# A gated FFN behind an inducing-point attention: the l factor on ScalarE, a thinner first output projection, a split last block

## The chip, the cores and the metric

The kernel runs on one core of one Trainium2 chip. The metric is the device time of one execution in microseconds (us); of the runs of a kernel the median counts. The core's engines are named as in the profile: PE (TensorE matmul; PEld is its weight load), DVE (VectorE), ACT (ScalarE), POOL (GpSimd) and SP (SyncE, which here only issues DMAs).

## The reference

Two blocks stand one behind the other. The first is attention through 32 inducing points `I`: `h = softmax(scale · I xᵀ) x` over all 12416 rows of a batch, then `out = softmax(scale · x hᵀ) h` for each row. The second is a gated FFN over all 49664 rows. Cut to what matters:

```python
B, N, m, C = (4, 12416, 32, 128)          # d_ff = 1536
def mab(q, kv):
    s = scale * (q @ kv.transpose(0, 2, 1))
    s = s - s.max(-1, keepdims=True)
    a = np.exp(s)
    a /= a.sum(-1, keepdims=True) + 1e-09
    return a @ kv
x = mab(x, mab(I, x)).reshape(B * N, C)
gate = 1.0 / (1.0 + np.exp(-(x @ w_gate)))
out = gate * (x @ w_val) @ w_out           # float32
```

## The kernel before

**Stage 1 and the first combine.** A batch is 97 chunks of 128 rows, taken in groups of 16 chunks and one group of one. For batch 0 all of stage 1 runs alone at the start: scores of the 32 inducing points against a group (L178), the negated maximum (L190), the exponential (L203), a transpose on PE (L216) that DVE copies out (L222), and the weighted sum of x rows (L236). Each group has its own maximum, so the groups are put together at the end (L559 to L625). There `ml` is the extreme of a partition's late groups, `wl` their weights (L562, ACT), `lsum` the weighted sum of the denominators (L596 and L598, DVE) and `hpart` the weighted sum of the numerators (four `scalar_tensor_tensor` at L603, DVE, each reading what the one before it wrote). The four 32-partition strips have separate extremes; POOL brings them together in `quad` (L566 to L576), ACT and POOL copy the result to all strips as `top` (L581, L583), and ACT forms the strip weight `w4` (L586) and `e32w` = `e32`·`w4` (L588). `e32l` = `e32`·`w4`·`lsum` is formed by DVE (L613) between the third and the fourth L603. Two fp32 matmuls then add up the strips: `l_ps` from `e32l` (L622) and `h_ps` from `hpart` and `e32w` (L624). `l_inverse` (L281, L283) and `h_take` (L288) give `hT`, from which the scores of the second attention (L362) and `hw`, h times both weight matrices (L294), are made. In this way the attention's second product and the two first FFN products become one matmul with 32 rows of contraction.

**The main loop.** The output is cut into 97 blocks of four chunks, 512 rows (the last block holds the one left-over chunk of each batch). A block has 12 slices of d_ff, done in 8 steps of alternately two slices and one: 776 steps in all. For step t, `product(t)` issues the value matmuls (`v_ps`, L696) and one DVE instruction `u = (t16 + 1) · v` (L717); `gate(t + 2)` issues the gate matmuls (`g_ps`, L696) and the tanh on ACT (L711). Steps with two slices use PSUM tiles of two banks (`g2`, `v2`), those with one slice one bank (`g1`, `v1`); each exists once, so the next value matmul into `v2` waits until DVE has read the last. Two steps are called a slot here: after the even step `beside` issues stage 1 and stage 2 work of what is to come, and after the odd step `project` issues output matmuls. One output chunk is four 128-column matmuls into `acc` (L733) that use one slice of one step's `u` as weights; a block takes 12 of them, after which ACT scales `acc` into `o32` (L745) and SP stores 256 KB (L748, for the last block L750). `project` does at most three chunks a slot, four if more than three wait, and stops behind a block's last chunk; in a steady state it is three a slot, twelve matmuls. The order of the instructions on each engine is the order in which this Python code issues them.

**PSUM.** The eight banks are `g2` (2), `v2` (2), `g1`, `v1`, `acc` and `m`; `m` serves the work of `beside`.

Of the kernel before, what the change touches and what calls it, by code (L numbers as in the profile page):

```python
# [9 lines left out]
F32 = mybir.dt.float32  # L10
# [3 lines left out]
ALU = mybir.AluOpType  # L14
AX = mybir.AxisListType

P = 128
GC = 16
BC = 4
# [2 lines left out]
S1_FIRST = 7  # L22
S2_LEAD = 20
COMBINE_LAG = 6


@with_exitstack
def kernel(
# [9 lines left out]
    nc = tc.nc  # L38
    B, N, C = x.shape
    m = inducing.shape[0]  # L40
    F = moe_w_gate.shape[1]
    NJ = F // P
# [11 lines left out]
    const = ctx.enter_context(tc.tile_pool(name="const", bufs=1))  # L54
# [7 lines left out]
    op = ctx.enter_context(tc.tile_pool(name="op", bufs=4))  # L62
# [3 lines left out]
    ps = ctx.enter_context(tc.tile_pool(name="ps", bufs=1, space=bass.MemoryType.PSUM))  # L66

    xv = x.rearrange("b (p j) c -> b p j c", p=P)
    ov = out.rearrange("(b p j) c -> b p j c", b=B, p=P)
    ov0 = out.rearrange("(b p j) c -> p j b c", b=B, p=P)  # L70
# [18 lines left out]
    def x_transpose_dma(b, s):  # L89
# [16 lines left out]
        out=identf[:],  # L106
        in_=identf[:],
# [21 lines left out]
    e32 = const.tile([P, m], F32, tag="e32")  # L129
# [9 lines left out]
    NS = len(groups)  # L139
    arrival = [0, NG] + list(range(1, NG))  # L140
    at_col = {s: p for p, s in enumerate(arrival)}
    EARLY = NS - 4
    nml = const.tile([P, 1 + NS - EARLY], F32, tag="nml")
    l1l = const.tile([P, 1 + NS - EARLY], F32, tag="l1l")
# [23 lines left out]
    def s1_dims(s):  # L168
        n = groups[s][1]
        ng = min(4, n)  # L170
        return ng, n // ng, 32 * ng
# [40 lines left out]
    def s1_turn_pe(b, s, a1T, tag="m"):  # L212
        ng, w, R = s1_dims(s)
        aT = ps.tile([P, 4, P], F16, tag=tag, name="aT_ps")
        for k in range(w):
            nc.tensor.transpose(aT[:, k, 0:R], a1T[0:R, ts(k, P)], ident[0:R, 0:R])  # L216
        return aT

    def s1_turn_copy(s, aT):
        ng, w, R = s1_dims(s)  # L220
        a1 = s1p.tile([P, 4, P], F16, tag="a1")
        nc.vector.tensor_copy(out=a1[:, 0:w, 0:R], in_=aT[:, 0:w, 0:R])  # L222
        return a1
# [6 lines left out]
    def s1_sum(b, s, a1, tag):  # L230
        c0, n = groups[s]
        ng, w, R = s1_dims(s)
        hp = ps.tile([P, C], F32, tag=tag, name="hp_ps")
        for k in range(w):
            for g in range(ng):
                nc.tensor.matmul(  # L236
                    hp[32 * g : 32 * g + 32, :],
                    a1[:, k, 32 * g : 32 * g + 32],
                    xn[b][:, c0 + g * w + k, :],
                    start=(k == 0),  # L240
                    stop=(k == w - 1),
                )
        summed[b] += 1
        if b == 0 and at_col[s] > EARLY:
            return hp
        nc.scalar.copy(out=hsts[b % 2][0:R, at_col[s], :], in_=hp[0:R, :])
# [25 lines left out]
    def add_tree(x, k, out=None):  # L272
        while k > 1:
            r = k // 2
            o = x[:, 0:r] if k > 2 or out is None else out
            nc.gpsimd.tensor_tensor(out=o, in0=x[:, 0:r], in1=x[:, k - r : k], op=ALU.add)
            k -= r
# [25 lines left out]
    def combine(b):  # L303
# [5 lines left out]
        for g in range(4):  # L309
            nc.gpsimd.tensor_copy(out=quad[:, g, :], in_=nm1[32 * g : 32 * g + 32, :])  # L310
        for _ in range(COMBINE_LAG):
            yield
# [20 lines left out]
        add_tree(hx, NS)  # L333
        for _ in range(COMBINE_LAG):
            yield
# [165 lines left out]
    a1T, a1 = {}, {}  # L501
    nm1, l1, hst = nm1s[0], l1s[0], hsts[0]
    for p in range(-2, NS - 3):
# [11 lines left out]
        if p + 1 == EARLY - 1:  # L515
# [3 lines left out]
                out=nml[:, 0:1], in_=nm1[:, 0:EARLY], axis=AX.X, op=ALU.min  # L519
            )  # L520
            nc.scalar.activation(
                out=we[:], in_=nm1[:, 0:EARLY], func=AF.Exp, bias=nml[:, 0:1], scale=-1.0
            )
            lw = const.tile([P, EARLY], F32, tag="lwe")
# [21 lines left out]
    sc, sb, sa = arrival[-1], arrival[-2], arrival[-3]  # L546
# [8 lines left out]
    aT = s1_turn_pe(0, sa, a1T[sa])  # L555
# [5 lines left out]
    wl = const.tile([P, 1 + NS - EARLY], F32, tag="wl")  # L561
    nc.scalar.activation(out=wl[:], in_=nml[:], func=AF.Exp, bias=ml[:], scale=-1.0)  # L562
    nc.scalar.mul(out=hpart[0][:], in_=hpart[0][:], mul=wl[:, 0:1])
    quad = const.tile([m, 4], F32, tag="quad0")
    for g in range(4):
        nc.gpsimd.tensor_copy(out=quad[:, g : g + 1], in_=ml[32 * g : 32 * g + 32, :])  # L566
    nc.gpsimd.tensor_scalar(
        out=quad[:, 0:1],
        in0=quad[:, 0:1],
        scalar1=quad[:, 1:2],  # L570
        scalar2=quad[:, 2:3],
        op0=ALU.min,
        op1=ALU.min,
    )
    nc.gpsimd.tensor_scalar(
        out=quad[:, 0:1], in0=quad[:, 0:1], scalar1=quad[:, 3:4], scalar2=None, op0=ALU.min  # L576
# [7 lines left out]
    nc.gpsimd.dma_start(wo16[:], moe_w_out.rearrange("(j p) c -> p j c", p=P))  # L584
    w4 = const.tile([P, 1], F32, tag="w4")
    nc.scalar.activation(out=w4[:], in_=ml[:], func=AF.Exp, bias=top[:], scale=-1.0)  # L586
    e32w = const.tile([P, m], F32, tag="e32w")
    nc.scalar.mul(out=e32w[:], in_=e32[:], mul=w4[:])  # L588
    for g in range(3):
        x_load(1, g)  # L590

    a1[sa] = s1_turn_copy(sa, aT)
    a1[sb] = s1_turn_copy(sb, s1_turn_pe(0, sb, a1T[sb], "g2"))
    hps = [hst[:, EARLY, :], s1_sum(0, sa, a1[sa], "acc")[:]]
    lw = const.tile([P, 1 + NS - EARLY], F32, tag="lwl")
    nc.vector.tensor_mul(out=lw[:], in0=l1l[:], in1=wl[:])  # L596
    lsum = const.tile([P, 1], F32, tag="lsum0")
    nc.vector.reduce_sum(out=lsum[:], in_=lw[:], axis=AX.X)  # L598
    a1[sc] = s1_turn_copy(sc, s1_turn_pe(0, sc, a1T[sc], "v2"))
    hps.append(s1_sum(0, sb, a1[sb], "m")[:])  # L600
    hps.append(s1_sum(0, sc, a1[sc], "v1")[:])
    for k, hp in enumerate(hps):
        nc.vector.scalar_tensor_tensor(  # L603
            out=hpart[0][:],
            in0=hp,
            scalar=wl[:, 1 + k : 2 + k],
            in1=hpart[0][:],
            op0=ALU.mult,
            op1=ALU.add,
        )  # L610
        if k == len(hps) - 2:
            e32l = const.tile([P, m], F32, tag="e32l0")
            nc.vector.tensor_scalar(  # L613
                out=e32l[:],
                in0=e32[:],
                scalar1=w4[:],
                scalar2=lsum[:],
                op0=ALU.mult,
                op1=ALU.mult,
            )  # L620
    l_ps = ps.tile([P, m], F32, tag="g1", name="l_ps")
    nc.tensor.matmul(l_ps[:], ones[:], e32l[:], start=True, stop=True)  # L622
    h_ps = ps.tile([P, m], F32, tag="m", name="h_ps")
# [9 lines left out]
        out=nmx_a[:], in_=s2_a[:, 0:BC, :], axis=AX.X, op=ALU.max, negate=True  # L633
# [3 lines left out]
        out=low[:],  # L637
        in0=s2_a[:, 0:BC, :],
        in1=nmx_a[:].unsqueeze(2).to_broadcast((P, BC, m)),
        op=ALU.add,  # L640
# [34 lines left out]
    blocks = []  # L675
# [10 lines left out]
    NST = len(steps)  # L686
# [19 lines left out]
    def gate(t):  # L706
        if t < NST:
            st = steps[t]
            hidden_mm(st, "g")
            st["t"] = tp.tile([P, st["cnt"], 512], F16, tag=f"t{st['cnt']}", name="t16")  # L710
            nc.scalar.activation(out=st["t"][:], in_=st["g"][:], func=AF.Tanh, scale=0.5)  # L711

    def product(t):
        st = steps[t]
        hidden_mm(st, "v")
        st["u"] = up.tile([P, st["cnt"], 512], F16, tag=f"u{st['cnt']}", name="u16")
        nc.vector.scalar_tensor_tensor(  # L717
            out=st["u"][:], in0=st["t"][:], scalar=1.0, in1=st["v"][:], op0=ALU.add, op1=ALU.mult
        )

    acc = [None]
    queue = [(t, k) for t in range(NST) for k in range(steps[t]["cnt"])]
# [2 lines left out]
    def project(upto, now, room):  # L725
        while queue and queue[-1][0] < upto and room > 0:
            t, k = queue.pop()
            st = steps[t]
            j = st["j0"] + k
            if j == 0:  # L730
                acc[0] = ps.tile([P, BC, C], F32, tag="acc", name="acc_ps")
            for i in range(BC):
                nc.tensor.matmul(  # L733
                    acc[0][:, i, :],
                    st["u"][:, k, ts(i, P)],
                    wo16[:, j, :],
                    start=(j == 0 and i == 0),
                    stop=(j == NJ - 1),
                    skip_group_check=True,
                )  # L740
            room -= 1
            if j == NJ - 1:
                block = blocks[st["block"]]
                o32 = op.tile([P, BC, C], F32, tag="o32")
                nc.scalar.mul(out=o32[:], in_=acc[0][:], mul=0.5)  # L745
                if len(block) == 1:
                    b, c, nb = block[0]
                    nc.sync.dma_start(ov[b, :, c : c + nb, :], o32[:])  # L748
                else:
                    nc.sync.dma_start(ov0[:, 0, :, :], o32[:])  # L750
                if now < NST:
                    return

# [5 lines left out]
    for b in range(B):  # L759
        at = base[b]  # L760
        for s in range(1, NS):
            c, n = groups[s]
# [70 lines left out]
    def waiting(upto):  # L833
        n = 0
        for e in reversed(queue):
            if e[0] >= upto:
                break
            n += 1
        return n
# [3 lines left out]
    for t in range(NST):  # L843
        product(t)
        gate(t + 2)
        if t % 2 == 0:
            beside(t // 2)
        else:
            project(t - 1, t, 3 if waiting(t - 1) <= 3 else 4)
    project(NST, NST, 10**6)  # L850


# [28 lines left out]
```

## Time and profile before

| | |
|---|---|
| runs shown | 768.11, 768.52, 766.72 us; median 768.11 |
| profiled execution | 768.34 us, of which the span from first to last instruction is 766.5 |
| first value and gate matmuls of the main loop | 31.8 us from the span's start |
| last matmul, last eviction, last store issued | end at 762.34, 762.97 and 763.39 us |
| share of the span busy | DVE 96%, ACT 88%, PE 87%, POOL 36% |

The span splits into a start-up of about 32 us, in which stage 1 of batch 0 and the first combine run, the main loop of some 730 us, and a tail of 4.2 us behind the last matmul. In a line of the timeline the first number is the start, the second the length of the merged group, and the bracket tells the idle time of the engine ahead of it and what ended it. A row of a table of windows gives the window, its length, the busy time and the number of instructions of each engine, and then the granted PE clock, where 1.00 is full and 0.50 is half.

### The profile page before, as it was taken

The page shows a single profiled execution, that of the slowest core. Times are in us where ns is not written, and L with a number is a line of the kernel's source. Part 1 is how long each engine was busy: PE and PEld are TensorE (multiplying, and loading weights), DVE is VectorE, ACT ScalarE, POOL GpSimd, SP SyncE. Part 2 cuts the span into 40 slices and gives each one's busy share as a digit, 9 for nine tenths or more (in the row PEclk, how much of TensorE's full clock was granted, in tenths as well). Part 3 has the DMA queues.
Part 4 walks back from the last instruction along what each step waited for, and adds up shares of the span by engine and source line. Part 5 has one row for each costly group of instructions (what it writes and reads, how often), then busy time and mean ns, then how long its engine had stood idle before and what let it go on. Part 6 is the DMA issues. An engine that isn't in the chain of part 4 may idle for free.

```text
span 766.5 us, 20798 instructions
## 1 busy us (share of the span) xinstructions
PE 669.1 (87%) x8167; PEld 402.6 (53%) x8167; DVE 736.3 (96%) x911; ACT 672.4 (88%) x1008; POOL 275.7 (36%) x439
## 2 busy tenths in 40 slices
PE   6788889889888888989888888888998888888887
PEld 4445555555555455555555545555555555555554
DVE  4889999999999999999999999999999999999997
ACT  4689889899898989989998989989999989889896
POOL 3535050582350441545513504147335135135100
PEclk9689999999999999999999999999999999999999
DMA  8979752604249525244138342121221121231211
GB/s 168 154 144 181 149 83 84 112 29 98 71 92 178 115 63 112 57 97 86 49 78 158 88 89 63 49 57 36 78 57 49 52 68 41 58 69 34 67 43 43
DMA packets 117730, 65.16 MB, mean 85 GB/s; under 512 B 101344, under 2 KB 102016, under 8 KB 117632
## 3 DMA queue, kind: packets, MB, share of 16 engines
q1 hardware_dynamic: 112192, 49.94, 27.9%
q0 software_dynamic: 5440, 13.90, 11.1%
q8 instruction: 64, 1.05, 0.6%
q14 instruction: 34, 0.28, 0.1%
HBM read 27.80 MB, written 25.43 MB: 69 GB/s over the span
## 4 chain that ended last, share of the span: by engine, by line
DVE 34%; PE 28%; issue 20%; ACT 14%; POOL 4%; DMA 1%; ACTq 0%; DVEq 0%; POOLq 0%
DVE u L717 30%; PE acc_ps L733 11%; PE v_ps L696 11%; ACT t L711 10%; PE s_ps L362 2%; DVE nm L190 2%; DVE nmx L373 2%; ACT a1T L203 1%; PE g_ps L696 1%; ACT e L395 1%; ACT o L745 1%; PE xt_ps L494 1%; POOL near L427 1%; PE s_ps L386 1%; DMA xn<-in_x_dram 1%
## 5 line engine op out<-in xcount | busy, mean ns | idle before, releaser
L717 DVE SCALAR_TENSOR_TENSOR u<-t,v_ps 128x1024 f16<-128x1024 f16 (+1 forms) x776 | 692.2, 950 | 11.3 <-ACT t L711 3.4
L711 ACT ACTIVATE t<-g_ps 128x1024 f16<-128x1024 f32 (+1 forms) x776 | 598.2, 818 | 68.2 <-PE g_ps L696 53.8
L696 PE MATMUL v_ps<-a2r,hwt 32*128 32x512 f16 (+1 forms) x1188 | 292.8, 371 | 79.3 <-DVE u L717 76.3
L733 PE MATMUL acc_ps<-wo,u 128*128 128x128 f16 x4656 | 328.6, 220 | 1.1
L733 PEld LDWEIGHTS <-u 128*128 128x128 f16 x4656 | 262.7, 98 | 97.4 <-issue 95.6
L696 PE MATMUL g_ps<-a2r,hwt 32*128 32x512 f16 (+1 forms) x1188 | 296.1, 378 | 0.3
L696 PEld LDWEIGHTS <-hwt 32*128 32x128 f16 x2400 | 100.0, 91 | 214.6 <-issue 168.7
L377 POOL CAST hi<-nmx 128x16 bf16<-128x16 f32 (+2 forms) x28 | 5.5, 196 | 320.4 <-DVE nmx L373 288.1
L449 POOL TENSOR_TENSOR a2n<-e,rs 128x2048 f16<-128x2048 f16 (+2 forms) x28 | 86.9, 3105 | 8.3 <-DVE rs L421 3.5
L427 POOL TENSOR_TENSOR near<-sme,minus 128x16 f32<-128x16 f32 (+1 forms) x26 | 66.9, 2572 | 1.9
L745 ACT ACTIVATE o<-acc_ps 128x512 f32<-128x512 f32 x97 | 58.8, 606 | 4.1 <-PE acc_ps L733 4.1
L403 POOL TENSOR_TENSOR sum<-e 128x256 f32<-128x256 f16 (+1 forms) x27 | 16.2, 599 | 72.2 <-ACT e L395 72.2
L403 POOL TENSOR_TENSOR sum<-sum 128x128 f32<-128x128 f32 (+3 forms) x108 | 31.5, 292 | 8.5
L362 PEld LDWEIGHTS <-xT 128*128 128x128 f16 x388 | 13.6, 97 | 12.5 <-issue 12.4
L362 PE MATMUL s_ps<-hT,xT 128*128 128x32 f16 x388 | 18.2, 179 | 0.7 <-DVE hT L288 0.5
L373 DVE TENSOR_REDUCE nmx<-s_ps 128x16 f32<-128x512 f32 (+2 forms) x28 | 17.0, 607 | 0.0
L203 ACT ACTIVATE a1T<-s_ps,nm 128x512 f16<-128x512 f32 (+1 forms) x24 | 15.0, 627 | 1.7 <-DVE nm L190 1.7
L190 DVE TENSOR_REDUCE nm<-s_ps 128x1 f32<-128x512 f32 (+1 forms) x24 | 14.8, 615 | 0.9 <-PE s_ps L178 0.9
L83 POOL DMA_DIRECT2D xn<-in_x_dram x25 | 15.1, 613 | 1.1 <-POOLq L865 0.8
L395 ACT ACTIVATE e<-s_ps 128x512 f16<-128x512 f32 (+2 forms) x28 | 14.9, 533 | 0.6 <-PE s_ps L386 0.6
L498 ACT COPY xT<-xt_ps 128x1024 f16<-128x1024 f16 (+1 forms) x6 | 5.6, 940 | 8.1 <-PE xt_ps L494 8.1
L496 DVE COPY xT<-xt_ps 128x1024 f16<-128x1024 f16 (+2 forms) x8 | 4.7, 598 | 8.3 <-PE xt_ps L494 8.3
(105 smaller groups left out, 200.0 us busy)
## 6 DMA issues: line engine op xcount, KB each, us to landing
out_dram<-o SPq DMA_DIRECT2D x97, 256.0 KB, 2.4
xn<-in_x_dram POOLq DMA_DIRECT2D x19, 512.0 KB, 6.6
xn<-in_x_dram POOLq DMA_DIRECT2D x4, 544.0 KB, 6.3
a2r<-a2n SPq DMA_TRANSPOSE x29, 5.1
xn<-in_x_dram POOLq DMA_DIRECT2D x1, 384.0 KB, 13.9
wg<-in_moe_w_gate_dram POOLq DMA_DIRECT2D x1, 384.0 KB, 4.5
wv<-in_moe_w_val_dram POOLq DMA_DIRECT2D x1, 384.0 KB, 5.8
wo<-in_moe_w_out_dram POOLq DMA_DIRECT2D x1, 384.0 KB, 5.4
```

The lines of the kernel that those rows point to most:

```text
L190: nc.vector.tensor_reduce(out=nm[0:R, col], in_=s1[0:R, 0 : w * P], axis=AX.X, op=ALU.max, negate=True)
L203: nc.scalar.activation(out=a1T[0:R, 0 : w * P], in_=s1[0:R, 0 : w * P], func=AF.Exp, bias=nm[0:R, col], accum_out=l1[0:R, col],)
L362: nc.tensor.matmul(s2[:, j, :], xT[b][:, c + j, :], hT16[b][:], start=(j == 0), stop=whole and j == j1 - 1, skip_group_check=True,)
L373: nc.vector.tensor_reduce(out=nmx[:, 0:n], in_=s2[:, 0:n, :], axis=AX.X, op=ALU.max, negate=True)
L403: nc.gpsimd.tensor_tensor(out=d[:, 0:n, :], in0=src[:, :, 0:w], in1=src[:, :, w : 2 * w], op=ALU.add)
L427: nc.gpsimd.tensor_tensor(out=near[:, 0:n], in0=sme[:, 0:n], in1=minus1[:, 0:n], op=ALU.pow)
L449: eng.tensor_tensor(out=a2n[:, 0:n, :, :], in0=e.unsqueeze(2).to_broadcast((P, n, 4, m)), in1=rs.unsqueeze(2).unsqueeze(3).to_broadcast((P ...
L696: nc.tensor.matmul(pt[:, k, col : col + nb * P], hw[b][r : r + 32, j // 2, :], a2r[r : r + 32, o : o + nb, :].rearrange("p j t -> p (j t)" ...
L711: nc.scalar.activation(out=st["t"][:], in_=st["g"][:], func=AF.Tanh, scale=0.5)
L717: nc.vector.scalar_tensor_tensor(out=st["u"][:], in0=st["t"][:], scalar=1.0, in1=st["v"][:], op0=ALU.add, op1=ALU.mult)
L733: nc.tensor.matmul(acc[0][:, i, :], st["u"][:, k, ts(i, P)], wo16[:, j, :], start=(j == 0 and i == 0), stop=(j == NJ - 1), skip_group_chec ...
L745: nc.scalar.mul(out=o32[:], in_=acc[0][:], mul=0.5)
```

## The change

Three edits.

1. **First combine.** The PE transposes, copies and sums of the groups `sa` and `sb`, and with them `lw` and `lsum`, are written ahead of the `quad` part. ACT then forms `e32s` = `e32`·`lsum` ahead of its copies of `top`, and `e32l` = `e32s`·`w4` right behind `w4` and ahead of `e32w`. The DVE instruction that formed `e32l` is gone. The orders on PE and POOL stay the same; DVE loses the one instruction; ACT gains two of 128x32.
2. **Output chunks.** While t < COLD = 8, `project` does at most one chunk a slot. The first odd step, t = 1, has no chunk yet, so three slots (t = 3, 5, 7) have one chunk in place of three. The chunks left over are done in later slots of four: on PE the slots from t = 3 on have 4, 4, 4, 16, 16, 4, 16, 16, 16, 16, 16, 16 output matmuls, where each had 12; from t = 27 on both orders are the same.
3. **Last block.** The last step's `u` is made by two DVE instructions of 256 columns. The last block accumulates in two PSUM banks (`acc` for the first two chunks, `m` for the other two). ACT evicts one and SP stores it, DVE evicts the other and ACT's queue issues its store.

```diff
+COLD = 8
...
     nc.scalar.mul(out=hpart[0][:], in_=hpart[0][:], mul=wl[:, 0:1])
+    a1[sa] = s1_turn_copy(sa, aT)
+    a1[sb] = s1_turn_copy(sb, s1_turn_pe(0, sb, a1T[sb], "g2"))
+    hps = [hst[:, EARLY, :], s1_sum(0, sa, a1[sa], "acc")[:]]
+    lw = const.tile([P, 1 + NS - EARLY], F32, tag="lwl")
+    nc.vector.tensor_mul(out=lw[:], in0=l1l[:], in1=wl[:])
+    lsum = const.tile([P, 1], F32, tag="lsum0")
+    nc.vector.reduce_sum(out=lsum[:], in_=lw[:], axis=AX.X)
+    e32s = const.tile([P, m], F32, tag="e32s")
+    nc.scalar.mul(out=e32s[:], in_=e32[:], mul=lsum[:])
...
     nc.scalar.activation(out=w4[:], in_=ml[:], func=AF.Exp, bias=top[:], scale=-1.0)
+    e32l = const.tile([P, m], F32, tag="e32l0")
+    nc.scalar.mul(out=e32l[:], in_=e32s[:], mul=w4[:])
     e32w = const.tile([P, m], F32, tag="e32w")
...
-        if k == len(hps) - 2:
-            e32l = const.tile([P, m], F32, tag="e32l0")
-            nc.vector.tensor_scalar(
-                out=e32l[:],
-                in0=e32[:],
-                scalar1=w4[:],
-                scalar2=lsum[:],
-                op0=ALU.mult,
-                op1=ALU.mult,
-            )
...
-        nc.vector.scalar_tensor_tensor(
-            out=st["u"][:], in0=st["t"][:], scalar=1.0, in1=st["v"][:], op0=ALU.add, op1=ALU.mult
-        )
+        cuts = [0, 512] if t < NST - 1 else [0, 256, 512]
+        for c, e in zip(cuts, cuts[1:]):
+            nc.vector.scalar_tensor_tensor(
+                out=st["u"][:, :, c:e],
...
             if j == 0:
-                acc[0] = ps.tile([P, BC, C], F32, tag="acc", name="acc_ps")
+                acc[0] = [ps.tile([P, BC, C], F32, tag="acc", name="acc_ps")]
+                if st["block"] == len(blocks) - 1:
+                    acc[0].append(ps.tile([P, BC, C], F32, tag="m", name="acc_ps"))
             for i in range(BC):
                 nc.tensor.matmul(
-                    acc[0][:, i, :],
+                    acc[0][(i // 2) % len(acc[0])][:, i, :],
...
-                    start=(j == 0 and i == 0),
+                    start=(j == 0 and i in ((0, 2) if len(acc[0]) > 1 else (0,))),
...
+            if t == NST - 1:
+                o32 = op.tile([P, BC, C], F32, tag="o32")
+                nc.scalar.mul(out=o32[:, 0:2], in_=acc[0][0][:, 0:2], mul=0.5)
+                nc.sync.dma_start(ov0[:, 0, 0:2, :], o32[:, 0:2])
+                nc.vector.tensor_scalar_mul(out=o32[:, 2:4], in0=acc[0][1][:, 2:4], scalar1=0.5)
+                nc.scalar.dma_start(ov0[:, 0, 2:4, :], o32[:, 2:4])
+            elif j == NJ - 1:
...
-            project(t - 1, t, 3 if waiting(t - 1) <= 3 else 4)
+            project(t - 1, t, 1 if t < COLD else 3 if waiting(t - 1) <= 3 else 4)
```

More of the change, by code (lines that the diff above doesn't have):

```diff
@@ L590 @@
         x_load(1, g)
[L592 to L598, printed above, removed]
     a1[sc] = s1_turn_copy(sc, s1_turn_pe(0, sc, a1T[sc], "v2"))
@@ L716, in product @@
         st["u"] = up.tile([P, st["cnt"], 512], F16, tag=f"u{st['cnt']}", name="u16")
-        nc.vector.scalar_tensor_tensor(
-            out=st["u"][:], in0=st["t"][:], scalar=1.0, in1=st["v"][:], op0=ALU.add, op1=ALU.mult
-        )
+        cuts = [0, 512] if t < NST - 1 else [0, 256, 512]
+        for c, e in zip(cuts, cuts[1:]):
+            nc.vector.scalar_tensor_tensor(
+                out=st["u"][:, :, c:e],
+                in0=st["t"][:, :, c:e],
+                scalar=1.0,
+                in1=st["v"][:, :, c:e],
+                op0=ALU.add,
+                op1=ALU.mult,
+            )
     acc = [None]
@@ L741, in project @@
             room -= 1
-            if j == NJ - 1:
+            if t == NST - 1:
[5 more added lines that the diff above has]
+            elif j == NJ - 1:
                 block = blocks[st["block"]]
                 o32 = op.tile([P, BC, C], F32, tag="o32")
[L745 to L750, printed above, removed]
+                nc.scalar.mul(out=o32[:], in_=acc[0][0][:], mul=0.5)
+                b, c, nb = block[0]
+                nc.sync.dma_start(ov[b, :, c : c + nb, :], o32[:])
                 if now < NST:
```

## The prediction

> **What bounds the kernel now.** I read the page's busy times and its clock row first, then windows laid along the changes of the clock, then the timelines of DVE and PE where it is half, the chain of waits through the first combine, and the last instructions.
>
> ```profile
> PE 669.1 (87%) x8167; PEld 402.6 (53%) x8167; DVE 736.3 (96%) x911; ACT 672.4 (88%) x1008; POOL 275.7 (36%) x439
> ...
> PEclk9689999999999999999999999999999999999999
> ...
> 25.45:35.69 10.24, 7.01 (x55) 2.95 (x55) 7.75 (x21) 5.06 (x10) 5.26 (x7) 0.50 1.01 162
> 35.69:39.11 3.42, 3.42 (x32) 1.90 (x31) 2.77 (x5) 1.88 (x4) 1.01 (x3) 0.50 1.14 197
> 39.11:42.52 3.41, 3.41 (x21) 1.50 (x22) 2.70 (x3) 2.56 (x4) 0.00 (x0) 0.50 1.21 224
> 42.52:45.93 3.41, 2.82 (x38) 1.78 (x36) 2.86 (x4) 2.88 (x6) 2.15 (x6) 1.00 0.62 113
> ```
>
> The main loop is DVE's (96%), and all three edits lie outside it: in the start-up, in the first slots and in the tail. The windows show the granted clock at 0.50 from 25.45 to 42.52 us, and there, from 35.69 on, PE is busy all the time (3.42 of 3.42) while DVE is not. So the first slots are PE's.
>
> ```profile
> 38.77 1.82 DVE L717 SCALAR_TENSOR_TENSOR u<-t,v_ps 128x1024 f16<-128x1024 f16 x2 [0.65 <-PE g_ps L696]
> 41.13 1.22 DVE L717 SCALAR_TENSOR_TENSOR u<-t,v_ps 128x1024 f16<-128x1024 f16 x1 [0.54 <-PE g_ps L696]
> 42.64 0.69 DVE L717 SCALAR_TENSOR_TENSOR u<-t,v_ps 128x512 f16<-128x512 f16 x1 [0.28 <-ACT e L395]
> 43.75 2.99 DVE L717 SCALAR_TENSOR_TENSOR u<-t,v_ps 128x1024 f16<-128x1024 f16 x3 [0.43 <-PE g_ps L696]
> ...
> 39.02 1.46 PE L733 MATMUL acc_ps<-wo,u 128*128 128x128 f16 x12
> 40.41 0.61 PE L696 MATMUL v_ps<-a2first,hwt 32*128 32x512 f16 x2
> ...
> 746.22 0.84 PE L733 MATMUL acc_ps<-wo,u 128*128 128x128 f16 x12
> 747.07 0.39 PE L696 MATMUL v_ps<-a2r,hwt 32*128 32x512 f16 x2
> ```
>
> DVE stood idle 0.65 + 0.54 + 0.28 + 0.43 = 1.90 us there. Twelve output matmuls hold PE for 40.41 - 39.02 = 1.39 us at half clock (116 ns each) and 747.07 - 746.22 = 0.85 at full clock less the gap before the next group, which I take as 65 ns each.
>
> **Edit 1, the first combine.** The chain of waits runs through the fourth L603, `l_ps` and the inverse to `hT`:
>
> ```profile
> 25.81 0.06 DVE e32l L613
> 25.86 0.06 issue
> 25.93 0.45 DVE hpart L603
> 26.37 0.11 issue
> 26.48 0.62 PE l_ps L622 x2
> ...
> 24.84 0.39 ACT L581 COPY top<-quad 32x1 f32<-32x1 f32 x2 [0.44 <-POOL quad L575]
> 25.32 0.30 ACT L586 ACTIVATE w<-ml,top 128x1 f32<-128x1 f32 x1
> 25.65 0.32 ACT L588 ACTIVATE e32w<-e,w 128x32 f32<-128x32 f32 x1
> ```
>
> The row of L613 gives 0.615 us for the one `e32l`: from 25.72 it ends at 26.33, and `l_ps` starts 0.15 behind it, at 26.48. After the change `e32l` takes `e32w`'s place on ACT, 25.65 to 25.97 by that row, and `l_ps` starts at 26.11: -0.37. What else `hT` needs does not hold it: the fourth L603 loses 0.08 (from 25.93 to 25.85) and ends at 26.26; `e32w` is pushed behind `e32l` to about 26.25; `h_ps` goes 0.42 behind `l_ps`, at 26.53, and ends at 27.14, before `li` at 27.33. The added wait is `e32s` on ACT for `lsum`, which DVE ends at 24.37. Behind it in ACT's queue stand the two copies of `top`, `w4`, `e32l`, `e32w` and, from 29.01, `e_a`. `e32s` would run 24.42 to 24.74 (0.32 as `e32w`), and the copies wait for POOL's `quad` until 24.84 in any case; the cover is 0.10 us, and what exceeds it delays `w4` one for one. The instructions written earlier keep their order on PE, DVE and POOL, so no queue but ACT's changes. Bounds: -0.40 to -0.08 (the L603 share alone). I take -0.37, because `l_ps` then waits for ACT and for nothing DVE ends later.
>
> **Edit 2, the first slots.** The half-clock slot around 40 us is PE's sum: 2 + 2 matmuls 0.40 (38.05 to 38.45), 1 + 1 matmuls 0.57 (to 39.02), twelve output matmuls 1.39 (to 40.41), 2.36 in all, which is the distance of DVE's rows (38.77 to 41.13). With four output matmuls PE needs 0.40 + 0.57 + 0.46 = 1.43. DVE needs 1.77 for its two instructions (the distance of 746.22 and the next such group, 747.99), so the slot turns DVE's. The gain cannot exceed the 1.90 us of DVE's idle time. Not all comes back: at half clock the refill of `v2` (0.61 and two hand-overs, some 0.75) is longer than the one-slice `u` that covers it (0.60), so 0.15 a slot stays, and the stretch at 41 us still has `beside`'s two L386 (0.97). I take 1.3 (bounds 0.9 and 1.9).
>
> The 24 matmuls come back at full clock, four extra in each of eight slots, 8 × 4 × 65 ns = 2.1 us of PE. In a full-clock slot the refill at 747.07 ends at 747.46 and the one-slice `u` that covers it ends at 747.52: about 0.1 of the 0.26 is hidden, and 0.16 stays, unless DVE has other work in that slot (`rs` at 48.4, `nm` at 50.3). Eight slots lose 1.3 at most, none at best; I take five, 0.8. Sum: -0.5, bounds +0.4 and -1.9. DVE's and SP's orders hardly move: the first block's store goes behind one transpose issue on SP, and the `o32` scaling moves some four tanhs back on ACT; nothing waits for that store.
>
> All this holds if the full clock comes back when it does now. PE being busy does not decide it: 35.69 to 39.11 is as full as 39.11 to 42.52, but only behind the second is the clock 1.00. What differs is what ran: each has about twelve output matmuls, which use all 128 rows of the array (L696 uses 32), but the second also has the two full-row L386 of 512 columns. The change takes two thirds of the output matmuls out of these stretches and leaves the L386 in. By full-row work the new second stretch lies between the one that failed and the one that did not, so I cannot exclude a return one stretch later.
>
> The Trainium skill (TensorE: Matmul & The Clock Gate, What's actually happening) says that the clock is judged in free-running windows of 4096 cycles at 1.2 GHz, 3413 ns, and that one busy window gives it back. The trace agrees on the length, as the 17.07 us at 0.50 are five times 3.41, and disagrees on "busy", since 35.69 to 39.11 was full and did not give it back. By the page's rule PE, which stays busy from slot to slot, would have its clock back no later than now, and the sum would stay; its advice in the table "Why this matters for your kernels", to keep PE busy without a break, speaks against thinning these slots.
>
> **Edit 3, the tail.** Now: the last `u` 761.20 to 761.88, its four matmuls 761.94 to 762.34, then these two rows, and landing 2.3 us later (L750).
>
> ```profile
> 762.38 0.60 ACT L745 ACTIVATE o<-acc_ps 128x512 f32<-128x512 f32 x1 [2.57 <-PE acc_ps L733]
> 763.00 0.40 SPq L750 DMA_DIRECT2D out_dram<-o  x1
> ...
> 763.50:764.00 0.50, 0.00 (x0) 0.00 (x0) 0.00 (x0) 0.00 (x0) 0.00 (x0) 1.00 0.08 24
> 764.00:764.50 0.50, 0.00 (x0) 0.00 (x0) 0.00 (x0) 0.00 (x0) 0.00 (x0) 1.00 1.00 289
> 764.50:765.00 0.50, 0.00 (x0) 0.00 (x0) 0.00 (x0) 0.00 (x0) 0.00 (x0) 1.00 0.75 212
> ```
>
> From L717's means at 1024 and 512 columns (1.220 and 0.679) a 256-column half takes 0.41 and follows the first by 0.34, so the second ends at 761.95 and bank `m`'s last matmul, of two in place of four, at 762.29; bank `acc` is done at 762.15, behind the chunk before it. ACT's half (1.030 and 0.606 at 1024 and 512 columns, so 0.39) ends at 762.57 and SP issues at 762.60, 0.40 earlier. DVE's half (0.41) ends at 762.74 and ACT issues at 762.77, 0.23 earlier. The windows show the old store as 0.9 us of full DMA load starting 0.95 behind its issue; both halves share these engines, so the new load starts 0.40 earlier and is as long: -0.40. DVE's eviction also waits for eight DMA semaphores, all long set, which can pass while the two `u` halves run. Bounds: -0.6 (DMA load halved on the last leg) and +0.25 (an ACT issue that costs the 0.61 of POOL's L83 in place of 0.395, and 0.26 for semaphores not covered, less the 0.23). I take -0.4, since the store's load is in a row of this trace.
>
> **Sum.** -0.37 - 0.5 - 0.4 = -1.27. Against the profiled execution, 768.34 us (span 766.5 and 1.84 around it), 767.07. That execution is 0.23 above the median 768.11, so a median of 766.8 is forecast.
>
> **The rivals.**
> 1. *Clock back one stretch later* (25%). For: the balance of full-row work above. Against: slots of sixteen are denser than any of now. In 3.41 us of half clock a slot of sixteen takes 0.40 + 0.57 + 16 × 0.116 = 2.83 in place of 1.77 + 0.16 = 1.93: 1.2 slots, +1.1 us. Time 767.9.
> 2. *Slower than before: clock stays half for two or three stretches more* (12%), at the place where the sixteens run, 43 to 53 us. It decides if full-row work below that of 39.11 to 42.52 never gives the clock back. +2.2 to +3.3, less 1.27: 768.8 to 769.9, in the middle 769.3.
> 3. *Little of it arrives* (15%): `e32s` runs into the `top` copies (-0.1), the repayment is the full 1.3 (0), and the second queue's issue eats the tail (-0.1): 767.9. For: a cover of only 0.10 us. Against: POOL's `quad` sets that time.
> 4. *More arrives* (10%): all of DVE's 1.9 idle us return and half the repayment hides under DVE's other work, -1.3, with -0.37 and -0.6: -2.3, 765.8.
> 5. *The change does less than it says*: in its "first four slots" t = 1 has no chunk to hold back. It is three, and counted so.
>
> **How the numbers follow.** Forecast 38%. The range 765.3 to 769.2 takes in rivals 1, 3, 4 and the lower half of 2, and 0.5 us of scatter below, the runs shown lying 1.8 us apart. A measurement of this kernel tells about 0.3%, 2.3 us, from no change: faster means below 765.8, slower above 770.4. Half of rival 4 and the scatter of the forecast make 14%, the upper end of 2 makes 7%, the rest, 79%, is no difference.
>
> **What would show it.** Right: `l_ps` near 26.1 and waiting for ACT; L717's idle before 43 us down to some 0.6 and new gaps of 0.1 to 0.2 in slots of sixteen; clock back at the same stretch; the last store's load 0.4 earlier. Wrong: a clock of 0.50 beyond 43 us, a `top` later than 24.9, or a last landing set by ACT's issue.

## The result and the profile after

Over 22 runs of each, the median went from 767.46 to 768.65 us: ratio 1.0014, with a 95% interval of 1.0008 to 1.0021. That is 1.2 us slower by the medians and 1.1 by the ratio, where 1.27 us faster was forecast. Later runs of both kernels beside each other on one chip gave 768.36 and 769.35, ratio 1.0011 (1.0001 to 1.0022).

The profiled execution of the changed kernel took 768.23 us with a span of 766.2. It is shorter than the median, and mid-loop times of the two profiled executions drift against each other by some 1 us, so the stages have to be read one by one. The windows, laid along the changes of the clock, come first (window, length, busy time of PE, PEld, DVE, ACT and POOL, granted clock, DMA share, GB/s):

```profile
22.80:36.46 13.66, 11.16 (x123) 5.32 (x124) 10.84 (x29) 8.45 (x22) 7.16 (x15) 0.50 0.86 143
36.46:39.87 3.41, 3.05 (x19) 1.02 (x18) 3.24 (x6) 2.11 (x4) 1.01 (x3) 0.50 1.20 211
39.87:43.28 3.41, 3.41 (x21) 1.20 (x20) 2.36 (x3) 2.82 (x4) 1.44 (x4) 0.50 1.19 224
43.28:46.70 3.42, 3.42 (x31) 2.39 (x30) 2.45 (x4) 2.15 (x4) 0.72 (x3) 0.50 1.13 160
46.70:50.11 3.41, 2.57 (x31) 1.36 (x30) 3.00 (x5) 2.69 (x5) 1.01 (x1) 1.00 0.22 50
```

The clock was at half for 23.89 us, seven stretches of 3.41, where the kernel before had five. It fell 2.65 us earlier than there (22.80 for 25.45) and came back 4.18 us later (46.70 for 42.52); what was added at the far end lies under the thin slots and the first slots of sixteen. The timeline of DVE shows what that did (start, length of the merged group, and in the bracket the idle time before it):

```profile
37.08 2.40 DVE L714 SCALAR_TENSOR_TENSOR u<-t,v_ps 128x512 f16<-128x512 f16 x3
39.65 1.22 DVE L714 SCALAR_TENSOR_TENSOR u<-t,v_ps 128x1024 f16<-128x1024 f16 x1 [0.17 <-PE v_ps L691]
41.52 0.69 DVE L714 SCALAR_TENSOR_TENSOR u<-t,v_ps 128x512 f16<-128x512 f16 x1 [0.65 <-ACT e L396]
42.61 1.82 DVE L714 SCALAR_TENSOR_TENSOR u<-t,v_ps 128x1024 f16<-128x1024 f16 x2 [0.40 <-PE g_ps L691]
45.40 1.82 DVE L714 SCALAR_TENSOR_TENSOR u<-t,v_ps 128x1024 f16<-128x1024 f16 x2 [0.97 <-PE g_ps L691]
47.63 1.22 DVE L714 SCALAR_TENSOR_TENSOR u<-t,v_ps 128x1024 f16<-128x1024 f16 x1 [0.41 <-PE g_ps L691]
```

The first gap, 0.65 in the kernel before, is gone, and the second shrank from 0.54 to 0.17, while the third, ahead of the one-slice `u` that waits for ACT, grew from 0.28 to 0.65. In their place stand 0.97 and 0.41 behind the two slots of sixteen, which ran at half clock. The ends of single products, after against before, give the account: step 3 is 0.38 us earlier (edit 1), step 6 1.48 earlier, step 7 1.11 earlier, step 12 0.34 later, step 27 1.01 later. From there to step 99 the difference stays at 1.0.

The first combine and the tail, as the chain of waits and the timeline show them:

```profile
26.31 0.36 DVE hpart L608
26.67 0.14 issue
26.80 0.62 PE h_ps L619 x2
27.42 0.02 issue
27.45 0.20 DVE hT L289
```

```profile
24.32 0.32 ACT L573 ACTIVATE e32s<-e,lsum 128x32 f32<-128x32 f32 x1
24.75 0.39 ACT L591 COPY top<-quad 32x1 f32<-32x1 f32 x2
...
25.56 0.32 ACT L598 ACTIVATE e32l<-e32s,w 128x32 f32<-128x32 f32 x1
25.79 0.30 ACT L600 ACTIVATE e32w<-e,w 128x32 f32<-128x32 f32 x1
```

```profile
762.41 0.38 ACT L748 ACTIVATE o<-acc_ps 128x256 f32<-128x256 f32 x1 [2.30 <-PE acc_ps L737]
762.63 0.42 DVE L750 TENSOR_SCALAR o<-acc_ps 128x256 f32<-128x256 f32 x1 [0.38 <-PE acc_ps L737]
762.82 0.39 SPq L749 DMA_DIRECT2D out_dram<-o  x1
763.09 0.43 ACTq L751 DMA_DIRECT2D out_dram<-o  x1
```

`e32s` fits ahead of the `top` copies with 0.11 us to spare, and in this execution `hT` waits for `h_ps`, no longer for `l_ps` and the inverse. In the tail, the time from the start of the last step's first product (761.51, before 761.20) to the end of the span went from 5.27 to 4.74 us.

### The profile page after: what moved, and what is told of

Same layout as the page of the kernel before. It is cut to its first block, busy times and chain, and to the rows that moved or that the text cites. A ratio compares the mean times of both kernels' runs of the same rounds, so it can differ in the third digit from the quotient of the medians.

```text
span 766.2 us, 20807 instructions
## 1 busy us (share of the span) xinstructions
PE 670.2 (87%) x8167; PEld 402.2 (52%) x8167; DVE 736.0 (96%) x912; ACT 673.0 (88%) x1010; POOL 276.1 (36%) x439
## 3 DMA queue, kind: packets, MB, share of 16 engines
q1 hardware_dynamic: 111936, 49.81, 27.3%
q8 instruction: 64, 1.05, 0.6%
## 4 chain that ended last, share of the span: by engine, by line
DVE 33%; PE 27%; issue 20%; ACT 13%; POOL 4%; DMA 2%; ACTq 0%; DVEq 0%; POOLq 0%
DVE u L714 29%; PE acc_ps L737 12%; PE v_ps L691 11%; ACT t L706 10%; DMA xn<-in_x_dram 2%; PE s_ps L363 2%; DVE nmx L374 2%; DVE nm L191 2%; ACT a1T L204 1%; PE g_ps L691 1%; ACT e L396 1%; POOL near L428 1%; PE s_ps L387 1%; ACT o L755 1%; POOL xn L84 1%
```

## The experiments

Every ratio is to runs of the kernel before beside it on the same chip. The first four kernels take the change apart.

**Edit 2 alone** (`c2_slots`), the kernel before with

```diff
+COLD = 8
...
-            project(t - 1, t, 3 if waiting(t - 1) <= 3 else 4)
+            project(t - 1, t, 1 if t < COLD else 3 if waiting(t - 1) <= 3 else 4)
```

> Only the thin slots (edit 2). Theory: taking output matmuls out of the half-clock slots delays the return of the full clock by a stretch of 3.41 us and the repayment costs 0.16 in most of eight slots; from the two traces (products 1.11 to 1.48 us ahead before the return, 1.0 us behind at the 28th step, of which 0.38 the other way is edit 1) the net is +1.4 us against the kernel before, ratio about 1.0018, with a granted clock near 0.985. Rival: the late clock of that trace was chance and the thin slots are worth the -0.5 that was forecast; then the ratio is 0.9993 and the loss must come from edit 1 or 3.

Measured: 769.64 against 768.01, ratio 1.0030 (1.0008 to 1.0051). One of its eleven runs, 779.07 us at a granted clock of 0.845, pulls the ratio up; the medians alone give 1.0021. In its trace the clock is half for 23.89 us, as in the changed kernel; and against the kernel before the product of step 2 ends 0.09 us later, that of step 6 1.02 earlier and that of step 27 1.05 later. The loss is edit 2's.

**Edit 1 alone** (`c1_combine`) and **edit 3 alone** (`c3_tail`), the first and the last group of hunks of the change.

> Only the first combine (edit 1). Theory: -0.38 us (the product of step 0 ends 0.37 earlier in the changed kernel's trace), ratio 0.9995; hT at about 27.6 us and the first gate matmuls at 31.4. Rival: the earlier start only moves the main loop against the clock's stretches, and what was gained is lost at half clock: ratio 1.0000 or more.

> Only the last block (edit 3). Theory: the span behind the last step's product shrinks by 0.5 us and some 0.1 of it is lost outside the span, where the second queue is set up: -0.4 us, ratio 0.9995. Rival: the store on the second queue costs as much as it saves: ratio 1.0000, with the time around the span (us less span) 0.2 or more above that of the kernel before.

Measured: edit 1, 767.34, ratio 0.9990 (0.9981 to 0.9999); edit 3, 767.31, ratio 0.9991 (0.9982 to 0.9999). Both rivals fall, if narrowly, since both intervals end at 0.9999. In the trace of edit 1 the first product ends 0.57 earlier than in the kernel before, in that of edit 3 the time from the last step's first product on shrinks by 0.54 us. The time around the span is 1.80 us on average with edit 3 and 1.85 without, so edit 3 alone costs nothing there. In every kernel that has edits 1 and 3 together it is 1.92 to 1.96; where these 0.07 us or more come from stays open.

**Edits 1 and 3 without edit 2** (`c13_no_slots`), the changed kernel with the last line of the diff undone; it was run a second time beside the changed kernel on one chip.

> The changed kernel without the thin slots (edits 1 and 3). Theory: -0.8 us against the kernel before, ratio 0.9990, and so 1.9 us faster than the changed kernel; clock back where it is in the kernel before (cold from about 25 to 42.5, granted 0.988). Rival (the loss is in edits 1 or 3): no faster than the kernel before.

> Edits 1 and 3 alone once more, beside the changed kernel on the same chip. Theory: 1.9 to 2.4 us faster than the changed kernel and ratio about 0.9985 to the kernel before, granted clock 0.989 to 0.991. Rival: the two lie within 1 us of each other, and the difference seen was one of chips.

> The changed kernel once more, beside the next one on the same chip. Theory: ratio to the kernel before 1.0008 to 1.0021 as measured, granted clock 0.983 to 0.987.

Measured: 766.85, ratio 0.9985 (0.9976 to 0.9993), and 766.92, ratio 0.9983 (0.9974 to 0.9992), beside 769.35 for the changed kernel: 2.4 us apart on one chip. This version is faster than both kernels; against the one before it gains 1.2 to 1.4 us, where 0.8 was expected. Its windows at half clock and the first behind them:

```profile
27.72:34.55 6.83, 5.18 (x47) 1.68 (x44) 5.55 (x14) 3.99 (x8) 3.01 (x4) 0.50 1.23 189
34.55:37.96 3.41, 3.41 (x32) 1.91 (x29) 3.02 (x4) 2.10 (x4) 0.90 (x4) 0.50 1.05 207
37.96:41.37 3.41, 3.41 (x24) 1.44 (x19) 2.61 (x3) 2.33 (x3) 0.17 (x1) 0.50 1.27 249
41.37:44.79 3.42, 2.88 (x37) 1.83 (x37) 2.94 (x5) 3.04 (x6) 2.15 (x6) 1.00 1.14 170
```

Four stretches in place of seven. The granted clock averaged over a run shows that this is no single execution's chance: with thin slots (the changed kernel and edit 2 alone, 44 runs) no run is above 0.988, while 21 of the 22 runs of edits 1 and 3 alone are at 0.989 or more. A stretch at half clock takes 0.5 × 3.41 / 766 = 0.0022 off that average, so 0.991 stands for four stretches, 0.989 for five, and 0.987 to 0.985, where most of the runs with thin slots lie, for six or seven. The kernel before is mostly at 0.989 to 0.991, and there the stretch has its price: on one chip 14 runs at 0.991 have a median of 767.46 and 16 at 0.989 one of 768.29, 0.83 apart; on the two others the same difference is 0.56 and 0.53.

**Thin, but not thin in work** (`d1_dense_thin`): the chunks are deferred as in the change, but the holes are filled with matmuls that cancel.

```diff
+    nwo = const.tile([P, 3, C], F16, tag="nwo")
+    nc.gpsimd.tensor_scalar_mul(out=nwo[:], in0=wo16[:, 0:3, :], scalar1=-1.0)
...
+            if now < COLD:
+                for again in (wo16, nwo):
+                    for i in range(BC):
+                        nc.tensor.matmul(
+                            acc[0][0][:, i, :],
+                            st["u"][:, k, ts(i, P)],
+                            again[:, j, :],
+                            start=False,
...
```

> The changed kernel, with the thin slots filled up again: behind each single chunk eight more output matmuls, four with the same weights and four with their negative, so that they cancel in the sum. It has the thin slots' deferral and none of their thinness. Theory (the density of full-row matmuls decides when the full clock comes back): clock back as without thin slots, four or five stretches of 3.41 us after it fell, granted 0.989 to 0.991, no product early at t = 4 to 7, and the repayment paid at full clock: about +0.8 against edits 1 and 3 alone, so -0.4 against the kernel before. Rival (the deferral itself, or chance, makes the clock late): granted 0.984 to 0.987 as in the changed kernel, and +2 or more against the kernel before.

```profile
33.52:36.93 3.41, 3.41 (x34) 1.79 (x33) 3.04 (x5) 3.03 (x4) 2.29 (x2) 0.50 1.07 207
36.93:40.34 3.41, 3.41 (x29) 1.92 (x26) 2.48 (x4) 1.51 (x2) 1.03 (x3) 0.50 1.24 213
40.34:43.76 3.42, 3.40 (x41) 1.92 (x38) 3.03 (x4) 3.20 (x5) 1.43 (x3) 1.00 1.13 236
```

Measured: 768.07, ratio 0.9996 (0.9987 to 1.0006), granted 0.989 in the median; the -0.4 us expected is not seen. The clock is back at 40.34, after five stretches. So it is the missing work that keeps the clock low, not the deferral. The deferral costs by itself: from step 8 to step 27 the products fall 0.82 us behind, at full clock. Nor is the difference one of where the clock first falls. In the traces in which it falls near 23 us, it is half for seven stretches with the thin slots (the changed kernel, edit 2 alone) and for five without them or with the holes filled (edit 1 alone, this kernel). Where it falls between 27.3 and 28.7 us, it is five with all three thin slots (the changed kernel once more) and four in the five others, of which none has more than one thin slot there.

**The repayment alone** (`p1_warm_slots`): three thin slots at t = 99, 101 and 103, where the clock is full.

```diff
-            project(t - 1, t, 3 if waiting(t - 1) <= 3 else 4)
+            project(t - 1, t, 1 if 99 <= t < 105 else 3 if waiting(t - 1) <= 3 else 4)
```

> The kernel before with three thin slots of one chunk at t = 99, 101 and 103, where the clock is full, and the same repayment behind them. It measures the repayment alone: theory, 0.16 to 0.3 us in each slot of sixteen in which DVE has no other work, so +0.7 to +1.3 us, ratio 1.0009 to 1.0017, and products of later steps later than before by that much, with nothing gained at t = 99 to 103. Rival (repayment is hidden at full clock, as half of it was forecast to be): +0.2 or less.

Measured: 768.76 against 768.15, ratio 1.0004 (0.9995 to 1.0013), which alone decides nothing. In the trace, the product of step 99 is 0.75 us ahead of that of the kernel before, those of steps 101 to 105 are 0.94 ahead, and that of step 131 only 0.32. The thin slots gained 0.2, the repayment took 0.6, and 0.43 net is lost, where +0.7 to +1.3 was expected.

**A clock that does not fall** (`w1_warm`, `w2_warm_thin`): matmuls whose result nothing reads, two or three at a time, at six places from the first combine on and in each of the first two steps; first without, then with the thin slots.

```diff
+    def warm(n, tag="g2"):
+        pt = ps.tile([P, 512], F32, tag=tag, name="warm_ps")
+        for k in range(n):
+            nc.tensor.matmul(
+                pt[:],
+                ident[:],
+                xn[0][:, 4 * k : 4 * k + 4, :].rearrange("p j c -> p (j c)"),
+                start=True,
+                stop=True,
+            )
```

> Edits 1 and 3 without the thin slots, and eighteen matmuls of 128x512 whose result nothing reads, put where PE waits between 22 and 35 us. Theory (the clock falls because PE does too little full-row work there): the clock does not fall, or falls for fewer stretches; granted 0.994 or more; first gate matmuls up to 0.5 us earlier, and the first slots at 1.77 in place of 2.36: -1.5 to -2.5 us against edits 1 and 3 alone, ratio to the kernel before about 0.996. Rival (such matmuls do not count, or delay the chain): clock as before, and slower than edits 1 and 3 alone by up to 1 us.

> The changed kernel, thin slots included, with the same eighteen matmuls. Theory: at full clock the thin slots have nothing to gain and cost their repayment, +0.7 to +1.3 us against the same kernel without them. Rival: they gain 0.5 at any clock, and this is the faster of the two.

Without the thin slots, the windows of the first slots and of a later place:

```profile
15.63:32.70 17.07, 15.46 (x232) 8.50 (x225) 14.01 (x39) 11.77 (x32) 9.66 (x25) 1.00 0.86 136
32.70:36.11 3.41, 3.25 (x36) 1.45 (x36) 3.20 (x5) 2.97 (x5) 1.92 (x1) 1.00 1.08 215
36.11:39.53 3.42, 2.29 (x28) 1.26 (x25) 3.42 (x5) 2.16 (x4) 1.01 (x3) 1.00 1.16 186
...
513.98:517.39 3.41, 2.19 (x26) 1.24 (x22) 3.38 (x6) 3.29 (x6) 0.63 (x4) 1.00 0.20 77
517.39:520.80 3.41, 3.41 (x22) 1.54 (x20) 2.61 (x3) 2.12 (x4) 3.07 (x6) 0.50 0.02 5
```

With them:

```profile
14.43:31.50 17.07, 15.60 (x244) 8.79 (x241) 13.95 (x37) 11.61 (x31) 9.29 (x24) 1.00 0.87 138
31.50:34.91 3.41, 3.03 (x33) 1.14 (x28) 3.13 (x6) 2.88 (x4) 2.31 (x1) 1.00 1.07 216
34.91:38.32 3.41, 2.33 (x23) 1.07 (x19) 3.41 (x5) 3.25 (x5) 1.01 (x3) 1.00 1.11 194
38.32:41.74 3.42, 2.96 (x12) 0.72 (x11) 1.92 (x3) 1.77 (x3) 0.13 (x1) 0.50 1.67 259
41.74:45.15 3.41, 3.41 (x31) 1.98 (x28) 2.30 (x3) 1.86 (x3) 2.03 (x6) 0.50 0.72 141
```

The matmuls hold the clock through the start-up, and step 27 is 1.61 us ahead of the kernel before, 0.83 more than with edits 1 and 3 alone. With the thin slots in it, the clock falls at 38.32, behind the stretch that holds the first two of them, and step 27 is 0.55 behind: the thin slots do not only delay the full clock, they can lose it. Measured: 767.02, ratio 0.9993 (0.9976 to 1.0010) without, where about 0.996 was expected, and 769.14, ratio 1.0010 (0.9999 to 1.0020) with the thin slots. The first spreads from 765.5 to 771.6 and is not shown to be faster than edits 1 and 3 alone; of the 0.83 us won early, the stretch at half clock from 517.39 on took 1.4 back in the profiled execution (products from 1.75 ahead to 0.37 ahead). Its three runs above 770 are those with the lowest granted clock (0.991 to 0.993, all others 0.996 or more); why the clock was at half for longer in them stays open.

**One thin slot** (`t1_one_thin`), the changed kernel with `COLD = 4`.

> The changed kernel with COLD = 4: one thin slot (t = 3), repaid by slots of sixteen at t = 5 and t = 7. The number of output matmuls in the first three slots is 36 as before, so theory says that the clock comes back as without thin slots (granted 0.989 to 0.991), DVE gains at most its 0.65 us of idle time and pays up to 0.9 at half clock: 0 to +0.4 us against edits 1 and 3 alone, and about 1.5 to 2 faster than the changed kernel. Rival (any deferral makes it late): granted 0.984 to 0.987 and within 0.5 of the changed kernel.

Measured: a median of 767.38, 2.0 below the changed kernel on the same chip, granted 0.991 in the median, though four of eleven runs lie at 0.984 to 0.986. Against the kernel before the medians (768.36) and the ratio, 1.0001 (0.9991 to 1.0010), don't say the same, and no difference is claimed. In its trace the clock is half for four stretches; step 4 gains 0.74, and by step 8 0.07 of the 0.90 at step 3 is lost. A thin slot whose work is made up within about a stretch mostly kept the clock as it was, and gained nothing.

## Why the prediction was wrong

- **Edit 1** was put at -0.37 from rows of ACT. `e32l` ended at 25.88 by its row, the cover of 0.10 held (0.11), and the edit alone measured -0.67 with an interval from nearly 0 to -1.5. Right in mechanism. That `hT` would still wait for `l_ps` did not hold in the profiled execution, where the transposes ahead of the fourth `hpart` ran at half clock and `h_ps` came last. It held in the traces of edit 1 alone and of edits 1 and 3, where `l_ps` starts at 25.91 and 26.16 (forecast 26.11).
- **Edit 3** was put at -0.4 and measured -0.54 in the trace, -0.70 in the medians (interval from nearly 0 to -1.4). ACT's issue came 1.58 us behind the start of the last step's first product (forecast 1.57), SP's 1.31 (forecast 1.40). The DVE eviction's eight semaphore waits had passed by 761.35, ahead of the last half of `u`, and ACT's issue (0.43) stayed short of the 0.61 of the upper bound.
- **Edit 2** was put at -0.5, as 1.3 gained and 0.8 repaid. The gain was 1.1 by step 6 (steps 3 to 6, -0.38 to -1.48). What came back was not 0.8 but 2.5: 0.37 behind the two L387 matmuls (L386 in the kernel before), 1.45 in the first two slots of sixteen, at half clock for the most part, and 0.67 in the other six. At full clock alone the repayment is 0.6 to 0.82 by the two experiments on it, so that term was about right for full clock. "The 24 matmuls come back at full clock" was not.
- **The step that failed** is "All this holds if the full clock comes back when it does now". It was weighed, and the wrong side taken: 38% for the forecast (63% with rivals 3 and 4, which also leave the clock as it was), 25% for one stretch later, 12% for more. The evidence I gave for a close call, the full-row work of the two stretches, was the right kind; counted out, it was close and lay on the failing side. If each matmul counts its columns times the share of the 128x128 array that it uses, an output matmul and a value or gate matmul (512 columns, a quarter of the array) count 128 each, and L386 counts 512. By matmuls that start in the stretch, with its edges taken 0.01 us early, 35.69 to 39.11 of the kernel before has 2944 and stays at half, 39.11 to 42.52 has 3328 and the clock returns. In the changed kernel 36.46 to 39.87 has 2560, 39.87 to 43.28 has 2688, and 43.28 to 46.70 with its sixteens has 3456. The 2688 leaves out one L387, 512, that starts at 39.85 and runs in the stretch. The count can also be spread over the time that a matmul's columns take (107 ns for 128 columns at half clock, the distance of the output matmuls in these traces). Then 39.87 to 43.28 has 3069. The two stretches of the kernel before have 2920 and 3284 in this way, so it lies between them, as the prediction said, and the clock stayed at half. The 24 deferred matmuls are 3072, about what one stretch needs.
- **Rival 2 is nearest to what happened.** In the two profiled executions the clock is half for two stretches more, and by the granted clocks the runs with thin slots have about two more than those of edits 1 and 3 alone. The rival's condition, that full-row work below that of 39.11 to 42.52 does not give the clock back, fits the traces. Its sum was off: 766.8 with 2.2 to 3.3 more is 769.0 to 770.1, not 768.8 to 769.9. Edit 2 costs 1.6 us alone and 2.4 on top of edits 1 and 3, which is 2.1 to 2.9 more than the -0.5 forecast. With the 0.82 that the deferral costs at full clock, the 2.4 leave 1.6 us for two stretches, 0.8 each by this estimate; rival 1 had put 1.1. The three edits alone add up to +0.26 us and together give +1.0 to +1.2; the difference lies within the intervals and stays open.
- The Trainium skill's rule that a busy window gives the clock back (TensorE: Matmul & The Clock Gate, What's actually happening) would have kept the forecast; 39.87 to 43.28 was busy for all of its 3.41 us and did not give it back. The page's advice to keep PE busy without a break (its table Why this matters for your kernels) spoke against the thin slots, and they did lose time, but not by a break: PE was busy for all of 39.87 to 46.70.

## What to carry to other kernels

Taking work off an engine that is the bound at a low clock can keep the clock low: count what the array would still do per stretch before thinning it, and defer work only as far as the same stretch. An edit that helps under a condition (here, that the clock comes back on time) has to be run without the others; three edits in one bundle hid a gain of 1.2 to 1.4 us behind a loss of 2.4. Where a clock record runs on a grid that is free against the kernel, compare distributions of runs, not one profile with another.

## What the runs showed of the hardware that was not expected

One number sorts the clock's changes in the thirteen traces. Count for each stretch of 3.41 us the column equivalents as above, by the matmuls that start in it. From full clock, every stretch of 2816 or fewer was followed by half, and every one of 3008 or more by full; 2944 occurs on both sides. From half clock, later than 13 us, every stretch of 3104 or more was followed by full and every one of 2944 or fewer by half, with 3072 on both sides. These values are coarse: a matmul that starts within 0.02 us of an edge moves them by 128 to 512. Spread over the time that the columns take, as above (56 ns for 128 columns at full clock), the two sides part: from full clock, 2965 or fewer was followed by half and 3015 or more by full; from half, 3069 or fewer by half and 3284 or more by full. Even so, edges moved by 0.05 us change single values by up to 120, and in one direction put one stretch that was followed by half (3072) above two that were not. The limit is the same both ways to within about a tenth, and PE's busy time does not tell: 513.98 to 517.39 above fell with 2.19 us of PE busy and 2560, 36.11 to 39.53 held with 2.29 us and 3200, and 34.91 to 38.32 fell with 2.33 us and 2304. Before 13 us, where PE runs transposes, the clock also came up behind 2560 to 2848; that is left open. Five of the thirteen traces also have one stretch at half in the main loop, at 337.30 us or between 517.39 and 523.63, each behind a stretch of 2560 to 2944; by the products it cost 1.1 to 1.4 us. The main loop's full slot has 18 × 128 = 2304 in 1.77 us, 4440 a stretch; a thin one has 1280, 2470 a stretch.

The Trainium skill (TensorE: Matmul & The Clock Gate, What's actually happening) has the stretch right, 3413 ns and free against the kernel's start: the clock first came up between 10.45 and 15.63 us in these traces, and each later interval at half within the kernel is a multiple of 3.41.
